# Pooled attention feeding a slot mixture of experts: idle products ahead of the scores dropped, second weights in 512 columns, half-width stores and loads joined

## The chip, the core and the metric

The kernel runs on one core of one Trainium2 chip. The metric is the device time of one execution in microseconds (us); before the change it is 179.56 us, the median of 3 runs (179.48 to 179.72). One further execution was recorded by the hardware profiler, and every duration below is from that record.

The names of the engines: PE is TensorE (PEld its weight loads), DVE is VectorE, ACT is ScalarE, POOL is GpSimd, SP is SyncE. POOL and SP here mostly issue DMAs: POOL the loads that cast f32 to bf16 on the way, SP the stores of the output.

## The reference

Two stages; only the second one's result is returned.

```python
def _attn_ref(q, k, v):                       # 8 batches, 8 heads, 576 rows, 64 columns, f32
    k_p = k.reshape(B, H, 72, 8, D).mean(axis=3)
    v_p = v.reshape(B, H, 72, 8, D).mean(axis=3)
    scores = scale * np.matmul(q, k_p.transpose(0, 1, 3, 2))
    attn = softmax over the 72 pooled keys
    return np.matmul(attn, v_p)

def _moe_ref(x, phi, w1, w2):                 # x 4608x512, 8 experts of 4 slots, w1 512x1024, w2 1024x512
    logits = x @ phi                          # 4608 x 32
    d = softmax of logits over the rows       # dispatch
    slot_input = d.T @ x                      # 32 x 512, four rows for each expert
    for e in range(E):
        slot_out[e] = np.maximum(slot_input[e] @ w1[e], 0.0) @ w2[e]
    c = softmax of logits over the slots      # combine
    return c @ slot_out                       # 4608 x 512
```

## The kernel before

**Batches go in four pairs.** For a pair, `load_pair` (L68 to L71) brings k, q and v into one tile each of 128 x 72 x 64 bf16. All twelve tiles share a pool of four buffers (tag `big`, L59), so the fifth load waits until the first tile has been read, and so on. The order of the loads is written out on POOL (`manual_schedule`, L66): k, q and v of pair 0, then of pairs 1 to 3 (L162 to L166), with w1 of expert 0 behind pair 2, then w1 of experts 1 to 7 (L167), then w2 of experts 0 to 3 into the same four `big` buffers (L169), w2 of experts 4 and 5 into the two buffers of the transposed q (L65 pool, issued at the end of pair 2), and last w2 of experts 6 and 7 into the two buffers of `xs` (`load_last_w2`, L85 to L96).

**PE's work on a pair.** `prepare_kq` pools k by products with `pmat` (L192), transposes q (L207) and folds the pooled k (L218). `prepare_v` pools v and carries it into the value tile (L256). `score_unit` makes the scores (L265) and ACT their exponentials (L266). `u_tile` multiplies by the values (L278), and DVE divides (L283, L284). `combine` makes the logits (L290), the slot inputs `G_ps` (L296) and the transposed combine weights `cT` (L311). The steps of the next pair's preparation are handed out one by one among the score units of the present pair. Until the last pair is done, the order on PE, ACT, DVE and SP is the tile framework's own; only POOL's is by hand.

**Idle products.** `warm(n, ps)` (L115) issues n products of 128x128 zeros with 128x512 zeros, whose result nobody reads. There are 18 of them at the top (L120), three times 4 among the steps of `prepare_kq(0)` (L341 to L344), seven in the last pair's logits, and 8 and 6 among the second weights (L508, L512).

**The last part** (from L388 on) has its order written out on PE, ACT, DVE and SP as well. The first weights give `hT`, a 128x32 weight block for each expert and each of eight row blocks, in which only the expert's own slots are not zero. `second(e, c)` (L470) then sums, for one expert and one half of 256 output columns, eight products, spread over four groups of 32 PSUM partitions; the two halves have a PSUM tile each (`so_ps`, L468). The second weights of experts 6 and 7 are loaded in column halves: five of eight row blocks of expert 6 in full width (L91), then for each half the other three row blocks of expert 6 (L94) and expert 7 in two DMAs of four row blocks each (L96).

**The output.** It is written by `output(g, cols)` (L479) in twelve groups: six of 256 rows (two per partition) and six of 512 rows (four per partition). The first five groups (`NHALF`) go in halves: as soon as column half 0 of the slot outputs is there (`slots_out(0)`, L477), its five groups are multiplied (L491), scaled by DVE for even and ACT for odd rows (L495, L493) and stored; then comes half 1. A store of a half row block (`w < DM`) is issued by SP for every row r by itself, 128 partitions of 1 KB (L498). The remaining seven groups are made in full width, one store each (L500): one of 512 KB and six of 1024 KB.

```python
        for r in range(n):
            f_ps = ...                                   # product, L491
            # scale into o_sb[:, r] on ACT (odd r) or DVE
            if w < DM:
                nc.sync.dma_start(out=dst[:, r], in_=o_sb[:, r])
        if w == DM:
            nc.sync.dma_start(out=dst, in_=o_sb)
```

Of the kernel before, what the change touches and what calls it, by code (L numbers as in the profile page):

```python
# [8 lines left out]
FP = mybir.dt.float32  # L9
BF = mybir.dt.bfloat16  # L10
AF = mybir.ActivationFunctionType
ALU = mybir.AluOpType
# [6 lines left out]
def kernel(  # L19
# [10 lines left out]
    nc = tc.nc  # L30
# [4 lines left out]
    DM = H * D  # L35
    E = moe_w1.shape[0]
    F = moe_w1.shape[2]
    NS = moe_phi.shape[1]
# [10 lines left out]
    FJ = F // 128  # L49
# [12 lines left out]
    ps_m = ctx.enter_context(tc.tile_pool(name="ps_m", bufs=2, space=PSUM))  # L62
# [15 lines left out]
    w2_sb = [None] * E  # L78
# [6 lines left out]
    def load_last_w2(pool, tag):  # L85

        j = FJ - 3
        src = [moe_w2[e].rearrange("(p j) d -> p j d", j=FJ) for e in range(E)]
        for e in (E - 2, E - 1):
            w2_sb[e] = pool.tile([128, FJ, DM], BF, name=f"w2_{tag}", tag=tag)  # L90
        nc.gpsimd.dma_start(out=w2_sb[E - 2][:, 0:j], in_=src[E - 2][:, 0:j])  # L91
        for c in range(2):
            cols = slice(c * DM // 2, (c + 1) * DM // 2)
            nc.gpsimd.dma_start(out=w2_sb[E - 2][:, j:FJ, cols], in_=src[E - 2][:, j:FJ, cols])  # L94
            for rows in (slice(0, FJ // 2), slice(FJ // 2, FJ)):
                nc.gpsimd.dma_start(out=w2_sb[E - 1][:, rows, cols], in_=src[E - 1][:, rows, cols])  # L96

    k_sb, q_sb, v_sb = [None] * NP, [None] * NP, [None] * NP

# [4 lines left out]
    hT = persist.tile([128, E, FJ, NS], BF)  # L104
# [10 lines left out]
    def warm(n, ps):  # L115
        for _ in range(n):
            nc.tensor.matmul(out=ps, lhsT=zeros[:, 0:128], rhs=zeros, start=True, stop=True)  # L117

    warm_ps = ps_m.tile([128, 512], FP, name="warm_ps", tag="m")
    warm(18, warm_ps)  # L120
    dummy = consts.tile([128, 1], BF)
    nc.scalar.activation(out=dummy, in_=zeros[:, 0:1], func=AF.Exp)

# [21 lines left out]
    for r in range(2):  # L145
        rows = slice(r * D, (r + 1) * D)
        nc.vector.tensor_copy(out=iphi[rows, :, 0:D],
                              in_=ident[rows, rows].rearrange("p d -> p () d").to_broadcast([D, H, D]))
# [8 lines left out]
    so = persist.tile([128, DM], BF)  # L157
    recC = persist.tile([128, 1], FP)
# [18 lines left out]
    ps_u = att.enter_context(tc.tile_pool(name="ps_u", bufs=2, space=PSUM))  # L177
# [5 lines left out]
    def pool_stage(src, dst):  # L183

        dst = dst.rearrange("p n (r i) -> p r n i", r=NR)
        for r0 in range(0, NR, 4):
            nr = min(4, NR - r0)
            ps = ps_m.tile([128, 4, BH, NI], FP, name="pool_ps", tag="m")
            for r in range(nr):
                for t in range(0, POOL, 2):  # L190
                    tt = (r0 + r) * POOL + t
                    nc.tensor.matmul(out=ps[:, r].rearrange("p n i -> p (n i)"),  # L192
                                     lhsT=src[:, tt:tt + 2, :].rearrange("p t d -> p (t d)"), rhs=pmat,
                                     start=(t == 0), stop=(t == POOL - 2))
            nc.scalar.copy(out=dst[:, r0:r0 + nr], in_=ps[:, 0:nr])  # L195
            yield

    def prepare_kq(pair):

        kpar = kvpool.tile([128, BH, SP], BF, name="kpar")  # L200
        yield from pool_stage(k_sb[pair], kpar)
        qT[pair] = qpool.tile([128, BH, NU, NI], BF, name="qT", tag="qT")
        for n, t0 in enumerate(range(0, NU, 6)):
            ps = ps_m.tile([128, 6, BH, NI], BF, name="q_ps", tag="m")
            for t in range(6):
                tt = 2 * (t0 + t)
                nc.tensor.transpose(out=ps[:, t].rearrange("p n i -> p (n i)"),  # L207
                                    in_=q_sb[pair][:, tt:tt + 2, :].rearrange("p t d -> p (t d)"), identity=ident)
            dst = qT[pair][:, :, t0:t0 + 6, :].rearrange("p n t i -> p t n i")
            if n % 3 == 1:  # L210
                nc.scalar.copy(out=dst, in_=ps)  # L211
            else:
                nc.vector.tensor_copy(out=dst, in_=ps)  # L213
            yield
        kp[pair] = kvpool.tile([128, BH, SP], BF, name="kp", bufs=2)
        for n in range(0, BH, HQ):
            ps = ps_m.tile([128, HQ, SP], FP, name="fold_ps", tag="m")
            nc.tensor.matmul(out=ps, lhsT=fold.rearrange("p r d -> p (r d)"), rhs=kpar[:, n:n + HQ],  # L218
                             start=True, stop=True)
            nc.vector.tensor_copy(out=kp[pair][:, n:n + HQ], in_=ps)  # L220
            if n % H:
                yield
# [115 lines left out]
        for g in gens:  # L338
            yield from g

    junk = ps_u.tile([128, 512], FP, name="junk", tag="u")  # L341
    for n, _ in enumerate(prepare_kq(0)):
        if n in (2, 5, 8):
            warm(4, junk)  # L344
    place_phi()

    comb = None
# [1 line left out]
    for pair in range(NP):  # L349
        for qd in range(2):  # L350
# [32 lines left out]
            if pair == NP - 1 and qd == 0:  # L383
                load_last_w2(xpool, "xs")
# [7 lines left out]
    junk = spare[:, 0]  # L392
# [26 lines left out]
    for n in range(E // NG):  # L419
        for half in range(F // 512):  # L420
            cols = slice(half * 512, (half + 1) * 512)
            h_ps = ps_m.tile([128, 512], FP, name="h_ps", tag="m")
            for j in range(DJ):
                for g in range(NG):
                    e = n * NG + g
                    nc.tensor.matmul(out=h_ps[g * NS:(g + 1) * NS],
                                     lhsT=siT[:, j, e * E:(e + 1) * E].rearrange("p e s -> p (e s)"),
                                     rhs=w1_sb[:, e, j, cols], start=(j == 0), stop=(j == DJ - 1),
# [17 lines left out]
    for n in [2] * NSMALL + [4] * ((NO - NSMALL) // 2):  # L446
        row0 = sum(128 * g[1] for g in groups)
        step_ = n // 2
        rows = lambda r, c0=row0 // 2, s=step_: cT[:, r % 2, c0 + r // 2:c0 + 128 * s:s]
# [14 lines left out]
    ps_o = ctx.enter_context(tc.tile_pool(name="ps_o", bufs=1, space=PSUM))  # L464
    ps_f = ctx.enter_context(tc.tile_pool(name="ps_f", bufs=4, space=PSUM))
    CW = DM // 2
    halves = [slice(c * CW, (c + 1) * CW) for c in range(2)]
    so_ps = [ps_o.tile([128, CW], FP, name=f"so_ps{c}") for c in range(2)]  # L468

    def second(e, c):  # L470
        for fj in range(FJ):
            g = fj % NG
            nc.tensor.matmul(out=so_ps[c][g * NS:(g + 1) * NS], lhsT=hT[:, e, fj], rhs=w2_sb[e][:, fj, halves[c]],  # L473
                             start=(e == 0 and fj < NG), stop=(e == E - 1 and fj >= NG), skip_group_check=True)

    def slots_out(c):
        nc.vector.tensor_scalar(out=so[:, halves[c]], in0=so_ps[c], scalar1=recC, scalar2=None, op0=ALU.mult)  # L477

    def output(g, cols):  # L479

        w = cols.stop - cols.start
        row0, n, rows = groups[g]
        dst = out[row0:row0 + 128 * n].rearrange("(p r) c -> p r c", r=n)[:, :, cols]
        if n == 4:

            o_sb = w1_sb[:, g - NSMALL].rearrange("p j f -> p (j f)").bitcast(FP).rearrange("p (r c) -> p r c", r=n)
        else:
            o_sb = opool.tile([128, n, w], FP, name=f"o_sb{w}", tag=f"o{w}", bufs=2 if w == DM else 2 * NHALF)
        for r in range(n):
            f_ps = ps_f.tile([128, w], FP, name="f_ps", tag="f")  # L490
            nc.tensor.matmul(out=f_ps, lhsT=rows(r), rhs=so[:, cols], start=True, stop=True)  # L491
            if r % 2:
                nc.scalar.activation(out=o_sb[:, r], in_=f_ps, func=AF.Copy, scale=recR[:, g, r:r + 1])  # L493
            else:
                nc.vector.tensor_scalar(out=o_sb[:, r], in0=f_ps, scalar1=recR[:, g, r:r + 1], scalar2=None,  # L495
                                        op0=ALU.mult)
            if w < DM:
                nc.sync.dma_start(out=dst[:, r], in_=o_sb[:, r])  # L498
        if w == DM:
            nc.sync.dma_start(out=dst, in_=o_sb)  # L500


    junk = ps_m.tile([128, 512], FP, name="junk", tag="m")
    for e in range(E - 2):
        for c in range(2):
            second(e, c)
        if e == E - 3:
            warm(8, junk)  # L508
    for c in range(2):
        second(E - 2, c)  # L510
        if c == 0:
            warm(6, junk)  # L512
        second(E - 1, c)
        slots_out(c)
        for g in range(NHALF):
            output(g, halves[c])
    for g in range(NHALF, len(groups)):
        output(g, slice(0, DM))
# [30 lines left out]
```

## Time and profile before

| what | value |
|---|---|
| median of 3 runs | 179.56 us (179.48 to 179.72) |
| the profiled execution | 179.56 us |
| its span, first to last instruction | 177.8 us, so 1.76 us lie around it |
| PE busy | 141.4 us (80%) |
| DVE, ACT, POOL busy | 91.1, 81.0, 19.7 us |
| loads through POOL's queue | 30.94 MB written as bf16, 6800 packets |
| stores and one small load through SP's queue | 9.50 MB, 4032 packets |
| HBM read, written | 61.93 MB, 9.44 MB |
| mean granted clock of TensorE | 0.835 |

How to read it: times on a line are microseconds from the start of the span. A line of the time-ordered view gives start, duration, engine, line of the kernel, operation, output and input tile and how many instructions are merged; in square brackets stands how long the engine was idle before and what ended that. In the table by stretches, the DMA share is the mean busy time of the core's 16 DMA engines (it can pass 1, as packets overlap), and GB/s counts bytes as they are written, so a load that casts f32 to bf16 counts half of what it reads.

### The profile page before, as it was taken

Reading aid. Unit: us, or ns where it says so; the run is one execution under the profiler, and the core shown is the slowest. Engines: PE = TensorE matmul, PEld = TensorE weight load, DVE = VectorE, ACT = ScalarE, POOL = GpSimd, SP = SyncE. Lnnn points to the kernel's source line nnn. Section 1 sums busy time; section 2 is a strip of 40 time slices with the busy share of each in tenths; the row PEclk is TensorE's granted clock in tenths of the full one; section 3 lists DMA queues with packets and bytes.
Section 4 is the critical chain, followed back from the end, with each engine's and each line's share of the span. In section 5 each row is a group of like instructions: output and inputs, shape, how many; then the busy total and the mean of one; then the engine's idle time right before and its main releaser. Section 6 shows DMA issues by size and latency. Waiting matters only on the chain.

```text
span 177.8 us, 3538 instructions
## 1 busy us (share of the span) xinstructions
PE 141.4 (80%) x1467; PEld 88.1 (50%) x1469; DVE 91.1 (51%) x252; ACT 81.0 (46%) x146; POOL 19.7 (11%) x39
## 2 busy tenths in 40 slices
PE   7983898799999999999999997798971486887000
PEld 2453576554986567865675444553660233322000
DVE  5401703446378787877868629843530006799000
ACT  3031389366595697856978813110200005599000
POOL 6010111002101160111111002103111000000000
PEclk9998799755699999999999567569998598589755
DMA  5999999999999999999999999999999999789994
GB/s 73 207 218 216 215 216 216 219 212 220 209 224 213 218 214 217 214 216 216 212 218 219 208 221 218 210 216 218 216 214 218 198 195 194 267 288 420 424 415 206
DMA packets 10846, 40.64 MB, mean 229 GB/s; under 512 B 976, under 2 KB 6480, under 8 KB 6736
## 3 DMA queue, kind: packets, MB, share of 16 engines
q0 software_dynamic: 6800, 30.94, 85.9%
q1 hardware_dynamic: 4032, 9.50, 13.8%
q8 instruction: 11, 0.18, 0.4%
q14 instruction: 3, 0.02, 0.0%
HBM read 61.93 MB, written 9.44 MB: 401 GB/s over the span
## 4 chain that ended last, share of the span: by engine, by line
PE 52%; DMA 24%; ACT 10%; DVE 4%; issue 2%; POOL 0%; ACTq 0%; DVEq 0%
DMA w_xs<-in_moe_w_dram 13%; DMA q_sb<-in_q_dram 11%; PE sc L265 8%; PE pool_ps L192 8%; PE u_ps L278 7%; PE G_ps L296 6%; PE q_ps L207 5%; PE f_ps L491 4%; PE warm_ps L117 4%; ACT w_sb L493 3%; DVE xs L284 2%; PE lg_ps L290 2%; PE fold_ps L218 2%; PE junk L117 1%; ACT ex_1632 L266 1%
## 5 line engine op out<-in xcount | busy, mean ns | idle before, releaser
L284 DVE TENSOR_TENSOR xs<-u_ps,rec 128x384 bf16<-128x384 f32 x72 | 39.4, 551 | 1.6
L265 PE MATMUL sc<-qT,kp 64*72 64x288 bf16 x128 | 24.5, 328 | 0.8 <-ACT ex_1633 L266 0.4
L283 DVE RECIPROCAL rec<-u_ps 128x4 f32<-128x4 f32 x72 | 12.4, 175 | 20.1 <-PE u_ps L278 19.8
L207 PE MATMUL q_ps<-ident,q_sb 128*128 128x128 bf16 x144 | 13.7, 249 | 5.3 <-DMA q_sb<-in_q_dram 5.0
L213 DVE COPY qT<-q_ps 128x768 bf16<-128x768 bf16 x16 | 8.8, 551 | 16.4 <-PE q_ps L207 16.3
L491 PE MATMUL f_ps<-so,cT 128*128 128x512 bf16 (+1 forms) x46 | 13.0, 385 | 2.8 <-DVE so L477 1.3
L207 PEld LDWEIGHTS <-q_sb 128*128 128x128 bf16 x144 | 10.4, 112 | 7.4 <-DMA q_sb<-in_q_dram 5.3
L265 PEld LDWEIGHTS <-kp 64*72 64x72 bf16 x128 | 8.9, 111 | 8.9 <-issue 3.5
L296 PE MATMUL G_ps<-xs,ee 128*128 128x512 bf16 x36 | 11.7, 468 | 0.4 <-ACT ee L291 0.4
L192 PE MATMUL pool_ps<-pmat,v_sb 128*128 128x128 bf16 x144 | 11.1, 239 | 0.0
L211 ACT COPY qT<-q_ps 128x768 bf16<-128x768 bf16 x8 | 6.4, 799 | 9.8 <-PE q_ps L207 9.7
L195 ACT CAST kpar<-pool_ps 128x512 bf16<-128x512 f32 (+1 forms) x12 | 5.5, 485 | 10.4 <-PE pool_ps L192 10.3
L491 PEld LDWEIGHTS <-cT 128*128 128x128 bf16 x46 | 4.8, 107 | 10.7 <-issue 7.9
L117 PEld LDWEIGHTS <-zeros 128*128 128x128 bf16 x51 | 5.6, 116 | 9.2 <-issue 5.0
L192 PEld LDWEIGHTS <-v_sb 128*128 128x128 bf16 x144 | 9.7, 109 | 0.8 <-issue 0.3
L493 ACT ACTIVATE o_sb_2313<-f_ps,recR 128x256 f32<-128x256 f32 x1 | 0.5, 474 | 20.5 <-PE f_ps L491 20.5
L192 PE MATMUL pool_ps<-pmat,k_sb 128*128 128x128 bf16 x144 | 9.7, 219 | 0.1
L192 PEld LDWEIGHTS <-k_sb 128*128 128x128 bf16 x144 | 8.4, 98 | 1.1 <-DMA k_sb<-in_k_dram 0.5
L495 DVE TENSOR_SCALAR w_sb<-f_ps,recR 128x512 f32<-128x512 f32 x12 | 8.3, 750 | 0.3 <-PE f_ps L491 0.2
L477 DVE TENSOR_SCALAR so<-so_ps_2183,recC 128x256 bf16<-128x256 f32 x1 | 0.5, 485 | 15.3 <-PE so_ps_2183 L473 15.3
L493 ACT ACTIVATE w_sb<-f_ps,recR 128x512 f32<-128x512 f32 x12 | 8.2, 687 | 0.2 <-PE f_ps L491 0.2
L195 ACT CAST vpar<-pool_ps 128x512 bf16<-128x512 f32 (+1 forms) x12 | 5.6, 480 | 5.7 <-PE pool_ps L192 5.6
(165 smaller groups left out, 238.8 us busy)
## 6 DMA issues: line engine op xcount, KB each, us to landing
w_sb<-in_moe_w_dram POOLq DMA_DIRECT2D x8, 1024.0 KB, 30.1
out_dram<-w_sb SPq DMA_DIRECT2D x6, 1024.0 KB, 8.9
k_sb<-in_k_dram POOLq DMA_DIRECT2D x4, 1152.0 KB, 17.8
q_sb<-in_q_dram POOLq DMA_DIRECT2D x4, 1152.0 KB, 17.9
v_sb<-in_v_dram POOLq DMA_DIRECT2D x4, 1152.0 KB, 16.3
w_big<-in_moe_w_dram POOLq DMA_DIRECT2D x4, 1024.0 KB, 38.4
w_qT<-in_moe_w_dram POOLq DMA_DIRECT2D x2, 1024.0 KB, 35.3
w_xs<-in_moe_w_dram POOLq DMA_DIRECT2D x4, 256.0 KB, 21.2
```

What stands on the lines that cost most here:

```text
L117: nc.tensor.matmul(out=ps, lhsT=zeros[:, 0:128], rhs=zeros, start=True, stop=True)
L192: nc.tensor.matmul(out=ps[:, r].rearrange("p n i -> p (n i)"), lhsT=src[:, tt:tt + 2, :].rearrange("p t d -> p (t d)"), rhs=pmat, start=(t ...
L195: nc.scalar.copy(out=dst[:, r0:r0 + nr], in_=ps[:, 0:nr])
L207: nc.tensor.transpose(out=ps[:, t].rearrange("p n i -> p (n i)"), in_=q_sb[pair][:, tt:tt + 2, :].rearrange("p t d -> p (t d)"), identity= ...
L213: nc.vector.tensor_copy(out=dst, in_=ps)
L265: nc.tensor.matmul(out=ps[:, r, 0:S // 2], lhsT=kp[pair][rows, n], rhs=qT[pair][rows, n], start=True, stop=True)
L278: nc.tensor.matmul(out=ps[rows, hh], lhsT=ex[b][:, hh].rearrange("p r t -> p (r t)")[:, c:c + rows.stop - rows.start], rhs=vp[(2 * pair + ...
L283: nc.vector.reciprocal(out=rec, in_=ps[:, :, XW])
L284: nc.vector.tensor_tensor(out=xs[pair][:, t, qd * HQ:(qd + 1) * HQ, :], in0=ps[:, :, 0:XW], in1=rec.rearrange("p h -> p h ()").to_broadcas ...
L296: nc.tensor.matmul(out=ps, lhsT=ee[:, t].rearrange("p g s -> p (g s)"), rhs=x[:, t, :, 0:D], start=(t == 0), stop=(t == 8))
L491: nc.tensor.matmul(out=f_ps, lhsT=rows(r), rhs=so[:, cols], start=True, stop=True)
L493: nc.scalar.activation(out=o_sb[:, r], in_=f_ps, func=AF.Copy, scale=recR[:, g, r:r + 1])
```

## The change

1. The 18 idle products at the top and the 12 among the steps of `prepare_kq(0)` are gone. The later ones stay.
2. `so_ps` becomes one tile of 128x512 f32. For experts 0 to 5 `second` multiplies all 512 columns with one product for each row block: 48 products in place of 96. Experts 6 and 7 go by halves, as before.
3. Expert 7's half columns come in one DMA of eight row blocks (512 KB) in place of two of four (256 KB each): two DMAs in place of four.
4. A half-width group of output rows is stored by one DMA with both rows (256 KB) once both are scaled, in place of one DMA for each row (128 KB): 10 stores in place of 20.

```diff
@@ load_last_w2
-            for rows in (slice(0, FJ // 2), slice(FJ // 2, FJ)):
-                nc.gpsimd.dma_start(out=w2_sb[E - 1][:, rows, cols], in_=src[E - 1][:, rows, cols])
+            nc.gpsimd.dma_start(out=w2_sb[E - 1][:, :, cols], in_=src[E - 1][:, :, cols])
@@
-    warm_ps = ps_m.tile([128, 512], FP, name="warm_ps", tag="m")
-    warm(18, warm_ps)
@@
-    junk = ps_u.tile([128, 512], FP, name="junk", tag="u")
-    for n, _ in enumerate(prepare_kq(0)):
-        if n in (2, 5, 8):
-            warm(4, junk)
+    for _ in prepare_kq(0):
+        pass
@@
-    so_ps = [ps_o.tile([128, CW], FP, name=f"so_ps{c}") for c in range(2)]
+    so_ps = ps_o.tile([128, DM], FP, name="so_ps")
-    def second(e, c):
+    def second(e, cols):
         for fj in range(FJ):
             g = fj % NG
-            nc.tensor.matmul(out=so_ps[c][g * NS:(g + 1) * NS], lhsT=hT[:, e, fj], rhs=w2_sb[e][:, fj, halves[c]],
+            nc.tensor.matmul(out=so_ps[g * NS:(g + 1) * NS, cols], lhsT=hT[:, e, fj], rhs=w2_sb[e][:, fj, cols],
@@ output
-            if w < DM:
-                nc.sync.dma_start(out=dst[:, r], in_=o_sb[:, r])
-        if w == DM:
-            nc.sync.dma_start(out=dst, in_=o_sb)
+        nc.sync.dma_start(out=out[row0:row0 + 128 * n].rearrange("(p r) c -> p r c", r=n)[:, :, cols], in_=o_sb)
@@
     for e in range(E - 2):
-        for c in range(2):
-            second(e, c)
-        if e == E - 3:
-            warm(8, junk)
+        second(e, slice(0, DM))
+    warm(8, junk)
     for c in range(2):
-        second(E - 2, c)
+        second(E - 2, halves[c])
         if c == 0:
             warm(6, junk)
-        second(E - 1, c)
-        slots_out(c)
+        second(E - 1, halves[c])
+        slots_out(halves[c])
```

More of the change, by code (lines that the diff above doesn't have):

```diff
@@ L467, with slots_out @@
     halves = [slice(c * CW, (c + 1) * CW) for c in range(2)]
-    so_ps = [ps_o.tile([128, CW], FP, name=f"so_ps{c}") for c in range(2)]
-    def second(e, c):
+    so_ps = ps_o.tile([128, DM], FP, name="so_ps")
+    def second(e, cols):
         for fj in range(FJ):
             g = fj % NG
-            nc.tensor.matmul(out=so_ps[c][g * NS:(g + 1) * NS], lhsT=hT[:, e, fj], rhs=w2_sb[e][:, fj, halves[c]],
+            nc.tensor.matmul(out=so_ps[g * NS:(g + 1) * NS, cols], lhsT=hT[:, e, fj], rhs=w2_sb[e][:, fj, cols],
                              start=(e == 0 and fj < NG), stop=(e == E - 1 and fj >= NG), skip_group_check=True)
-    def slots_out(c):
-        nc.vector.tensor_scalar(out=so[:, halves[c]], in0=so_ps[c], scalar1=recC, scalar2=None, op0=ALU.mult)
+    def slots_out(cols):
+        nc.vector.tensor_scalar(out=so[:, cols], in0=so_ps[:, cols], scalar1=recC, scalar2=None, op0=ALU.mult)
     def output(g, cols):
@@ L482, in output @@
         row0, n, rows = groups[g]
-        dst = out[row0:row0 + 128 * n].rearrange("(p r) c -> p r c", r=n)[:, :, cols]
         if n == 4:
```

## The prediction

> **What bounds the kernel now.** I read the page's 40 slices first. From the third microsecond to the end the DMA engines are busy, so the time is what they have to move, plus every stretch in which they move it slowly.
>
> ```profile
> PEclk9998799755699999999999567569998598589755
> DMA  5999999999999999999999999999999999789994
> GB/s 73 207 218 216 215 216 216 219 212 220 209 224 213 218 214 217 214 216 216 212 218 219 208 221 218 210 216 218 216 214 218 198 195 194 267 288 420 424 415 206
> ```
>
> A slice is 4.45 us. Up to slice 33 loads run at some 216 GB/s written. At the end stores run at 420. Between them two slices have only 267 and 288, and DMA falls from 9 to 7 and 8 tenths: a hole in the work of the bounding resource. The table by stretches gives its size (duration, busy time of PE, PEld, DVE, ACT, POOL, then granted clock, DMA share, GB/s):
>
> ```profile
> 149.00:158.30 9.30, 8.23 (x40) 3.21 (x40) 7.24 (x14) 6.47 (x13) 0.00 (x0) 0.63 0.80 259
> 159.00:165.00 6.00, 4.14 (x14) 1.25 (x13) 5.29 (x8) 5.42 (x8) 0.00 (x0) 1.00 1.01 410
> 165.00:175.50 10.50, 0.00 (x0) 0.00 (x0) 0.00 (x0) 0.00 (x0) 0.00 (x0) 0.58 1.01 421
> ```
>
> What holds it back is SP, in order of time:
>
> ```profile
> 148.56 0.82 SPq L498 DMA_DIRECT2D out_dram<-o_sb_2313  x2
> 149.42 0.94 SPq L498 DMA_DIRECT2D out_dram<-o_sb_2322  x2
> ...
> 156.38 0.89 SPq L498 DMA_DIRECT2D out_dram<-o_sb_2402  x2
> 157.36 0.90 SPq L498 DMA_DIRECT2D out_dram<-o_sb_2411  x2
> 158.36 0.39 SPq L500 DMA_DIRECT2D out_dram<-o_sb_2420  x1
> 158.91 6.29 SPq L500 DMA_DIRECT2D out_dram<-w_sb  x6
> ```
>
> Twenty half-width stores go out from 148.56 to 158.36, one every 0.49 us, without a pause. 131,072 bytes per 0.49 us are 267 GB/s: the rate of the hole. Two more rows say that SP is the limit, not the engines or the data: each store lands 1.9 to 2.2 us after its issue, the first as the last, so none queues; and the last half rows are scaled by 154.78, 3 us before SP sends them.
>
> **The loads have slack everywhere.** The list of POOL's waits shows loads held for PE, but a load waits behind others in the queue anyway:
>
> ```profile
> 39.90 0.53 POOL L70 DMA_DIRECT2D v_sb<-in_v_dram  x1 [9.07 <-PE q_ps L207]
> ...
> 61.58 0.53 POOL L70 DMA_DIRECT2D v_sb<-in_v_dram  x1 [7.46 <-PE sc L265]
> ...
> 121.97 1.55 POOL L96 DMA_DIRECT2D w_xs<-in_moe_w_dram  x2 [10.38 <-PE G_ps L296]
> ```
>
> The load ahead of the first (q of pair 2, issued 30.30, 18.4 to landing) lands at 48.7, that ahead of the second (q of pair 3, 53.59 + 17.4) at 71.0: PE could be 8.8 and 9.4 us later, less about 1 us until data flow, before the engines run dry. These are the smallest margins. Expert 7's loads, issued at 121.97, land 23.8 us later. So PE, at 80%, sets no end before 146.7, when the last piece of half 0 lands.
>
> **Idle products (part 1).** PE's own order in time:
>
> ```profile
> 1.19 6.57 PE L117 MATMUL warm_ps<-zeros 128*128 128x512 bf16 x18 [1.19 <-DVE ones L136]
> 7.60 2.75 PE L117 MATMUL junk<-zeros 128*128 128x512 bf16 x12
> 10.37 2.18 PE L192 MATMUL pool_ps<-pmat,k_sb 128*128 128x128 bf16 x36
> 15.84 0.84 PE L207 MATMUL q_ps<-ident,q_sb 128*128 128x128 bf16 x12 [3.28 <-DMA q_sb<-in_q_dram]
> ...
> 32.28 0.84 PE L207 MATMUL q_ps<-ident,q_sb 128*128 128x128 bf16 x12 [1.74 <-DMA q_sb<-in_q_dram]
> ```
>
> All 30 lie before 10.37, where k lands (issued 1.24, 9.1 to landing). Taking them away saves nothing; that wait is their cover. They do leave a fast PE: their weight loads start 0.43 us apart until 6.28 and 0.21 after. Without them the 36 pooling products run at the slow rate, as 32 of pair 1's v did at clock 0.50 (3.48 us, 0.109 each): 3.9 us in place of 2.2. The 1.7 us more go into the 3.28 us wait for q; the q load of pair 1, released by them, goes out at 14.6 in place of 12.85, where the load ahead lands at 26.7. Cost 0. If PE stays slow to 30.5, its some 9.4 us of busy time from 20 on double; less the 1.74 us wait at 32.28 it is 7.7 us late, still inside the margins.
>
> The Trainium skill, "TensorE: Matmul & The Clock Gate", Part 1, says that PE starts at half rate and is released after a busy window of about 3.4 us. Here it took 5.1 us of idle products. The rule speaks against the change; by it the slow time would be less than the row's, and both give 0 behind the wait.
>
> **Second weights (part 2).** Eight 256-column products take 0.22 us start to start at full clock (131.44 to 131.66), so sixteen take 0.44. Eight of 512 columns are in no row; bounds are 0.22 (a product costs its issue) and 0.44 (its columns); I take 0.44. Either way PE then waits 1.94 and 4.22 us for experts 4 and 5. One PSUM bank for both halves could make half 1's writes wait for DVE's reading of half 0; but ten output products stand between and need what DVE wrote, so no wait is added. Cost 0.
>
> **Expert 7 in one DMA per half (part 3).** POOL issues two fewer. The second piece today goes out 0.8 us after the first and lands 23.9 later, so the joined one lands with it, at 146.7. But four products that run before that (at 145.77) now come after: half of 0.22, so +0.11 us on half 0. On half 1 PE is busy with expert 6 until about 150.4, when the last piece lands (135.33 + 15.1): +0 to 0.2, inside the next sum's rounding.
>
> **Joined stores (part 4)** is what counts. SP's issue for two rows of 1 KB per partition is in no row: all stores here have one piece per partition, and cost 0.33 to 0.45 us whether 128 or 512 KB. Bounds: 0.49 pitch as now, or 0.98 if it goes by pieces. POOL's rows lean to the first: 128 pieces 0.54, 512 pieces (L96) 0.77. I take 0.55. For the rate of 1 KB pieces the ends are 268 / 0.80 = 335 GB/s (the hole, scaled to a full share) and 416 (the full-width stores); I take 335, the same piece.
>
> From issue to flow I take 0.85 us: the last half store is issued at 157.86, and the bytes after 159.0 add up to 6.87 MB, about the 6.82 MB of the full-width stores, so it had flowed by 159.1 with 0.3 to 0.4 for its own bytes.
> - Half 0: first pair scaled at 148.60 + 0.11, issued 148.8, flows from 149.65. Pairs follow every 0.45, so SP and data outrun the engines: 1.31 MB at 335 are 3.9 us, to 153.55.
> - Half 1: first pair scaled at 152.69 + 0.11, issued 152.85, flows from 153.7 to 157.6.
> - Group 5 (0.52 MB, scaled at 156.06): 157.6 + 1.26 = 158.9.
> - Six full stores: the first is scaled at about 157.6, so ready to flow at 158.55; 158.9 + 6.29 MB / 416 = 174.0.
>
> Now the flow ends at 175.5: **1.5 us less**. At 416 GB/s throughout, the scaling of the first full group is late next (158.55), and the end is 173.65: 1.85 less. The profiled execution took 179.56, the median itself, so 179.56 - 1.5 = 178.06; I say 178.0.
>
> The Trainium skill, "DMA: Bandwidth & Descriptors", section "Issuing engines are not separate DMA queues", calls the sequencer's time to start a DMA usually small beside the DMA. Here 0.49 us of SP stands against 0.39 us of engine time. By the rule joining would save nothing, 179.6.
>
> **Rivals.**
> - Less of it: PE's clock is lower at the end (half-width products were 0.52 apart at clock 0.5, 0.45 at 1.0), or fuller stores hold back the last load at 150.4. Each moves the first full group by up to 1 us: 178.6 to 179.2. Chance 0.11.
> - Joining saves no issue time: 0.98 per joined store. SP sends from 148.75, ten times 0.98, group 5 at 158.55 in place of 158.36: 179.7. For it: no row with two pieces. Against: POOL's rows. Chance 0.13.
> - Slower, by the clock: PE, never brought up, stays at half rate past 47. For: it was at 0.50 from 34 to 47 though busy throughout. It decides where v of pair 2 or 3 goes out over 8 us late. 7.7 late at 32, and each busy microsecond after 47 adds one; slow to 55 gives 7.7 + 8 - 8.4 = 7 us of empty engines, 178 + 7 = 185. Against: 5 us of dense products brought the clock up, and pair 1's v did so at 47. With smaller mishaps of this kind 0.11.
> - The forecast's own case, 177.0 to 178.6: 0.65.
>
> **How the numbers follow.** A measurement here tells about 0.2% from no change, so faster is under 179.2 and slower over 179.9. Faster 0.65 + 0.11 = 0.76, same 0.13, slower 0.11. The range goes from 177.0 (stores at 416 and half a microsecond earlier in flow) to 179.8, the no-gain case, and leaves out the slow clock.
>
> **What would show it.** Ten joined stores about 0.55 apart, landing later than 2 us (a queue); no 267 in the slices after the loads; the first full store issued near 157.7; the last load where it was, about 150.4; pooling of k at 0.109 each and q of pair 1 still landing by 32.3. Joined issues near 1 us, or a DMA share under 9 tenths between 10 and 140 us, would prove it wrong.

## The result, and the profile after

The changed kernel takes 179.0 us (median of 6 runs, 178.75 to 179.08) against 179.64 us of the kernel before (6 runs, 179.48 to 180.48): ratio 0.9949, 95% interval 0.9925 to 0.9974. So it is faster, by some 0.5%. Its profiled execution took 179.02 us, with a span of 177.2. The forecast was 178.0: the right side, the right mechanism for the stores, and a third to a half of the size; what took the rest was not in it.

The slices of the page after, to be read against those of before:

```profile
PEclk9999999655599999999999858558999569999655
DMA  4999999999999999999999999999999999999993
GB/s 73 210 221 210 223 208 224 208 224 208 223 207 215 219 218 214 219 215 209 218 220 211 211 226 215 209 215 224 213 209 223 197 196 152 343 348 416 424 422 137
```

The two slices of 267 and 288 GB/s have become 343 and 348, and DMA is at 9 tenths there. A new low, 152, stands just ahead of them. SP in order of time (start, duration):

```profile
148.76 0.61 SPq L491 DMA_DIRECT2D out_dram<-o_sb_2230  x1
149.46 0.56 SPq L491 DMA_DIRECT2D out_dram<-o_sb_2238  x1
...
154.27 0.61 SPq L491 DMA_DIRECT2D out_dram<-o_sb_2311  x1
154.98 0.98 SPq L491 DMA_DIRECT2D out_dram<-o_sb_2319  x1
...
156.06 1.37 SPq L491 DMA_DIRECT2D out_dram<-o_sb_2327  x1
157.61 6.26 SPq L491 DMA_DIRECT2D out_dram<-w_sb  x6
```

Ten stores where there were twenty, 0.67 us apart (0.58 of issue and 0.1 between). But the tenth and the one behind it hold SP for 0.98 and 1.37 us, and the first full store, whose last row had been scaled by 156.3, goes out at 157.61. The table by stretches (busy time of PE, PEld, DVE, ACT, POOL, then clock, DMA share, GB/s) shows two holes, at 149 and at 157:

```profile
149.00:150.00 1.00, 0.81 (x9) 0.33 (x11) 0.98 (x4) 0.97 (x3) 0.00 (x0) 1.00 0.22 30
...
155.00:157.00 2.00, 1.80 (x7) 0.63 (x7) 2.00 (x4) 1.80 (x4) 0.00 (x0) 1.00 1.03 343
157.00:158.00 1.00, 0.80 (x4) 0.28 (x4) 1.00 (x2) 1.00 (x2) 0.00 (x0) 1.00 0.74 263
158.00:165.00 7.00, 3.81 (x14) 1.08 (x12) 4.98 (x8) 4.72 (x8) 0.00 (x0) 1.00 1.03 421
```

In the kernel before the microsecond from 149 on moved 180 GB/s. So far that is the forecast's sum with some terms off. What it had no term for shows in the completions. Every store is spread over sixteen DMA engines, and the trace has sixteen completions for each, in order of time here:

```
completions of a store, us:      first    8th     15th    last engine
before, last full store          175.89  176.00  176.07  176.10
after, 6th joined store          154.90  154.98  155.05  155.08
after, 7th                       155.67  155.75  155.84  156.49
after, 8th                       156.40  156.49  156.60  158.38
after, 10th                      157.91  158.00  158.10  159.72
after, last full store           174.56  174.66  174.76  175.57
```

From the seventh joined store on, one completion of the sixteen, so one engine, is up to 1.8 us late, and at the end still 0.8. What was on it? The DMA view of 155.9 to 157.0 in the changed kernel (queue, packets, MB, share of 16 engines) has a packet that belongs to no tile:

```profile
q1 hardware_dynamic: 378, 0.36, 97.2%
q8 instruction: 1, 0.02, 5.5%
```

It begins at 155.93 and is 16 KB of instructions: 5.5% of sixteen engines over 1.1 us are 0.96 us of one engine. The kernel before has its last such packet at 143.66, among the loads:

```profile
q0 software_dynamic: 410, 0.20, 137.1%
q8 instruction: 1, 0.02, 5.5%
```

Both kernels have eleven of these packets while they run; the page of before has them as one line:

```profile
q8 instruction: 11, 0.18, 0.4%
```

Counted in TensorE's weight loads and products, they come 255 apart on average in the kernel before (215 begun at the first, 2768 at the last); no other engine has more than 252 instructions in all on that page. The experiments below that change nothing but TensorE's products move the last packet. The Trainium skill, "Runtime: NRT & Kernel Launch", section "Instruction fetch mechanics", says that an engine's instructions are refilled in blocks of 16 KiB, 256 instructions; the trace agrees. The changed kernel has 78 products fewer (30 idle ones and 48 of the second weights), 156 instructions of the 2936 on the page. So the last block falls due later in the work, at 155.93. The trace doesn't name the DMA engine that carries a packet: that the late engine is the one with the packet is inferred from the times, and from the runs below.

### The profile page after: what moved, and what is told of

Read it like the earlier page. It is cut to its first block, busy times and chain, and to the rows that moved or that the text cites. A ratio compares the mean times of both kernels' runs of the same rounds, so it can differ in the third digit from the quotient of the medians.

```text
span 177.2 us, 3367 instructions
## 1 busy us (share of the span) xinstructions
PE 134.0 (76%) x1389; PEld 85.8 (48%) x1391; DVE 91.0 (51%) x252; ACT 80.4 (45%) x146; POOL 18.5 (10%) x37
## 4 chain that ended last, share of the span: by engine, by line
PE 48%; DMA 28%; ACT 10%; DVE 4%; issue 2%; ACTq 0%; DVEq 0%; POOLq 0%
DMA w_xs<-in_moe_w_dram 13%; DMA q_sb<-in_q_dram 10%; PE pool_ps L189 10%; PE sc L262 8%; PE u_ps L275 8%; PE G_ps L293 6%; PE q_ps L204 5%; DMA k_sb<-in_k_dram 5%; PE f_ps L485 3%; ACT w_sb L487 2%; DVE xs L281 2%; PE fold_ps L215 2%; PE lg_ps L287 2%; ACT ex_1600 L263 1%; ACT ex_1601 L263 1%
## 5 line engine op out<-in xcount | busy, mean ns | idle before, releaser
L189 PE MATMUL pool_ps<-pmat,k_sb 128*128 128x128 bf16 x144 | 11.6, 242 | 10.1 <-DMA k_sb<-in_k_dram 10.0
L204 PE MATMUL q_ps<-ident,q_sb 128*128 128x128 bf16 x144 | 14.5, 258 | 3.9 <-DMA q_sb<-in_q_dram 3.5
L189 PEld LDWEIGHTS <-k_sb 128*128 128x128 bf16 x144 | 10.1, 110 | 10.6 <-DMA k_sb<-in_k_dram 10.0
L204 PEld LDWEIGHTS <-q_sb 128*128 128x128 bf16 x144 | 11.1, 117 | 6.2 <-DMA q_sb<-in_q_dram 3.9
L485 PE MATMUL f_ps<-so,cT 128*128 128x512 bf16 (+1 forms) x46 | 11.0, 331 | 3.5 <-DVE so L472 1.2
L485 PEld LDWEIGHTS <-cT 128*128 128x128 bf16 x46 | 4.3, 96 | 10.0 <-issue 7.6
L472 DVE TENSOR_SCALAR so<-so_ps,recC 128x256 bf16<-128x256 f32 x2 | 1.0, 482 | 14.1 <-PE so_ps L468 14.1
L217 DVE CAST kp<-fold_ps 128x288 bf16<-128x288 f32 x16 | 7.0, 441 | 1.6 <-PE fold_ps L215 1.5
```

## The experiments

**Theory A:** the joined stores bring some 1.6 us, and about 1 us of it is lost because the missing instructions move a fetch from the loads in among the stores, where each engine has its fixed share of the last bytes. **Rival B:** the joined stores bring what is measured, and the fetch costs nothing. **Rival C:** the gain is another part's.

**1. Joined stores alone** (part 4 on the kernel before):

```diff
-            if w < DM:
-                nc.sync.dma_start(out=dst[:, r], in_=o_sb[:, r])
-        if w == DM:
-            nc.sync.dma_start(out=dst, in_=o_sb)
+        nc.sync.dma_start(out=dst, in_=o_sb)
```

> The kernel before with part 4 alone: half-width rows joined into one store. Theory A (a 16 KB instruction fetch of PE, which moves with the number of PE instructions ahead of it, holds one DMA engine back among the last stores, and cost the changed kernel some 1 us): PE's list is untouched, so the last fetch stays at 143.7 us, ahead of the stores, and all sixteen engines finish the last store together. 177.8 to 178.3 us. Rival B (joined stores bring only what the changed kernel shows, and the fetch costs nothing): 179.0. Rival C (the gain came from the wide products or the joined loads): 179.6.

Measured 178.43 us (178.04 to 178.76), ratio 0.9917 (0.9895 to 0.9939). The last fetch is at 143.6, and the last store completes on its first and last engine at 174.28 and 174.50. One part of the change beats the whole by the medians, though the two intervals still overlap a little. It is 0.13 us above A's range, but all six runs lie below B and C.

**2. The 30 idle products put back** into the changed kernel (part 1 undone):

> The changed kernel with its 30 idle products put back (part 1 undone). 60 PE instructions more move the last fetch from 155.9 to some 149.9 us, where the engines stand nearly empty between the loads and the first joined store. A: 178.0 to 178.7. B, and whoever holds that idle products cost nothing in any way: 179.0.

Measured 179.02 us, with a wide range of 178.42 to 179.62 (10 runs), ratio 0.9948 (0.9928 to 0.9967). The fetch came at 150.72, not in the hole but on the first joined store, one of whose engines completes 1.7 us after the others, and the issue of the third store took 1.72 us. In the profiled execution, the slowest of the ten, the last load, too, landed late on one engine (150.97 in place of 150.3). The median is B's 179.0 and outside A's range: a miss for A, and with this spread no decision by itself.

**3. Instructions alone: 64 idle products of 32 columns** at the top of the changed kernel:

```diff
+    warm_ps = ps_m.tile([128, 512], FP, name="warm_ps", tag="m")
+    for _ in range(64):
+        nc.tensor.matmul(out=warm_ps[:, 0:32], lhsT=zeros[:, 0:128], rhs=zeros[:, 0:32], start=True, stop=True)
     dummy = consts.tile([128, 1], BF)
```

> The changed kernel with 64 idle products of 32 columns at the top, for their number of instructions alone: 128 more move the last fetch to some 145 us, among the last loads. A: 177.8 to 178.3, one engine no longer behind the others at the last store. B: 179.0.

Measured 178.03 us (177.85 to 178.36), ratio 0.9899 (0.9878 to 0.9919); run again as the base of the last three, 178.0 (0.992, 0.9901 to 0.9938). Work added on PE makes the kernel 1 us faster. The fetch is back among the loads (DMA view of 143.9 to 144.9):

```profile
q0 software_dynamic: 371, 0.19, 137.4%
q8 instruction: 1, 0.02, 5.8%
```

SP is no longer held, and the first full store goes out 0.9 us sooner than in the changed kernel:

```profile
148.89 7.65 SPq L494 DMA_DIRECT2D out_dram<-o_sb  x11
156.71 6.99 SPq L494 DMA_DIRECT2D out_dram<-w_sb  x6
```

All engines complete the last store between 174.39 and 174.61. The clock in the store stretch is 1.00 in both kernels up to 164.9, so a warmer PE is not the reason. Nor do the added products reach the stores by another way: the last load lands at 150.43 (150.31 in the changed kernel), and the first store goes out at 148.89 (148.76).

**4. Fewer instructions still**: the changed kernel without the seven idle products of the last pair's logits, and with expert 6's first five row blocks in 512 columns. The diff is abridged: `second` also gets the row blocks as a third argument.

```diff
-    warm(2, junk)      # twice, and warm(3, junk), among the last logits
+    second(E - 2, slice(0, DM), range(FJ - 3))
     for c in range(2):
-        second(E - 2, halves[c])
+        second(E - 2, halves[c], range(FJ - 3, FJ))
```

> The changed kernel with fewer PE instructions still: without the seven idle products of the last pair's logits, and the first five row blocks of expert 6 multiplied in 512 columns, 24 instructions less. A: the list ends before the last fetch falls due, or the fetch comes so late that it meets the last full-width stores; without it 177.8 to 178.3, with it 179.0 to 179.5. B: 179.0.

Measured 179.61 us (179.42 to 180.06), ratio 0.9993 (0.9979 to 1.0007): the whole gain is gone. The fetch fell at 162.2, among the full stores:

```profile
q1 hardware_dynamic: 52, 0.42, 102.6%
q8 instruction: 1, 0.02, 5.9%
```

Fifteen engines complete the last store by 174.53, as in experiment 3 (174.59), and the sixteenth at 176.18. The expected range, up to 179.5, is missed by 0.1 us. One more thing differs from experiment 3: PE's clock was 0.50 from 149.6 to 156.4 here and 1.00 there. But experiment 1 had the same low clock, from 149.8 to 156.7, and sent its stores at the same times. Stores and one stretch of experiment 1, then of experiment 4:

```profile
148.65 7.89 SPq L497 DMA_DIRECT2D out_dram<-o_sb  x11
157.67 7.17 SPq L497 DMA_DIRECT2D out_dram<-w_sb  x6
153.00:155.00 2.00, 1.92 (x7) 0.76 (x6) 1.47 (x4) 1.46 (x4) 0.00 (x0) 0.50 0.96 324
...
148.71 7.85 SPq L488 DMA_DIRECT2D out_dram<-o_sb  x11
157.58 7.94 SPq L488 DMA_DIRECT2D out_dram<-w_sb  x6
153.00:155.00 2.00, 1.92 (x7) 0.76 (x6) 1.47 (x4) 1.51 (x4) 0.00 (x0) 0.50 0.95 324
```

In experiment 1 the fifteenth engine completes the last store at 174.48 and the sixteenth at 174.50. So B falls here: with less work and the same stores, one engine alone is late, and the kernel is 1.2 us slower than experiment 1 and 1.6 us slower than experiment 3.

**5. Single rows again**, on experiment 3 (part 4 undone):

> The third experiment (64 short idle products, last fetch at 143.9 us) with the half-width rows stored one by one again (part 4 undone). If the joined stores are the whole gain: SP sends twenty stores 0.49 us apart again, the first full store goes out near 158.9, 179.4 to 179.8 us. If the wide products or the joined loads brought some of it: 178.5 to 179.2.

Measured 180.1 us (179.44 to 180.28), ratio 1.0012 (0.9999 to 1.0025). SP sends twenty stores 0.49 us apart and the first full one at 159.26. The time is 0.3 us above the range of the first case, and on its side: parts 1 to 3 without part 4 bring nothing, and C falls. The stretch reads as that of before:

```profile
153.00:155.00 2.00, 1.53 (x7) 0.58 (x6) 1.92 (x5) 1.79 (x5) 0.00 (x0) 1.00 0.80 268
155.00:157.00 2.00, 1.79 (x7) 0.63 (x7) 2.00 (x4) 1.80 (x3) 0.00 (x0) 1.00 0.80 268
```

**6. Parts 1 and 2 alone** on the kernel before:

> The kernel before with parts 1 and 2 alone (no idle products at the top, experts 0 to 5 in 512 columns). The last fetch moves to some 156 us, among single-row stores, which leave each DMA engine 20% idle. Theory A1 (a fetch costs only where its engine has no idle time left to catch up): 179.5 to 179.9. A2 (a fetch among the stores costs the same 1.1 us or more wherever it falls): 180.5 or more.

Measured 180.68 us (180.54 to 181.29), ratio 1.0054 (1.0036 to 1.0072). A1 was mine, and it fell; the time is in A2's range. The fetch came at 154.68, and the engines' spare fifth did not help, since SP, the bound there, was held itself: one store's issue took 1.51 us in place of 0.40. The late engine had caught up by the end (the last store completes between 177.04 and 177.25 on all), but every store behind went out later, the first full one at 160.08 in place of 158.91. The same stretch as above:

```profile
153.00:155.00 2.00, 1.58 (x7) 0.68 (x7) 1.92 (x4) 1.79 (x4) 0.00 (x0) 1.00 0.83 273
155.00:157.00 2.00, 1.80 (x7) 0.58 (x6) 2.00 (x4) 1.79 (x4) 0.00 (x0) 1.00 0.36 116
```

**7. 18 short idle products** in place of experiment 3's 64:

> The changed kernel with 18 short idle products at the top: 36 PE instructions more put the last fetch at some 152 us, amid the joined stores and earlier than the changed kernel's 155.9. Theory A: still in the stretch where all engines are full, so 178.9 to 179.7, one engine's landings behind the others. Rival B: 179.0 as the changed kernel, with no engine behind. If only fetches in the last 20 us count: 178.0.

Measured 178.55 us (178.34 to 179.04), ratio 0.9936 (0.9918 to 0.9953), below the range. The fetch came at 151.72; one engine was 1.9 us late and had made up all but 0.4 by the end. The other fifteen end at 174.85, 0.4 us later than in experiment 1, which had the same low clock in this stretch: from 153 to 155 the engines moved 260 GB/s here and 324 there. By the medians the fetch cost 0.5 us against experiment 3 and 0.1 against experiment 1, and the interval overlaps those of both. That an early fetch costs less is suggested by this, not shown.

**8. The first group row by row**, on experiment 3, to start the first flow sooner:

> The third experiment with the first group of half 0 alone stored row by row. The first joined store's bytes flowed 1.3 us after its issue, a single row's 0.85 us. If the slow start of joined stores costs what the engines' empty stretch from 149 to 150.2 suggests, 0.3 to 0.5 us: 177.5 to 177.8. If the time is made up later, or the first full store is what is late: 178.0.

Measured 178.27 us (177.82 to 178.69), ratio 0.9914 (0.9894 to 0.9935). Not faster than experiment 3. In the profiled execution the last load landed at 150.78 on one engine and the first store went out 0.3 us later, so what the slow start costs stays open.

**10. Expert 7's loads in two pieces per half**, on experiment 3 (part 3 undone), beside experiment 9, its repeat:

> The third experiment once more, as the base of the next three on the same chip: 178.0 us (177.8 to 178.4).

> The third experiment with expert 7's half columns loaded in two pieces each again (part 3 undone). By the working of part 3 the joined load costs 0.11 us on half 0, hidden or not: 177.9 to 178.1, no difference that can be told. If the joined load holds back the last landing: 177.6 or less. If joining helped: 178.3 or more.

Measured 178.38 us (178.04 to 178.66) against 178.0 (177.91 to 178.84); the intervals of the ratios, 0.9915 to 0.9944 and 0.9901 to 0.9938, overlap. The median is in the range named for a joined load that helps, but part 3 can't be told from nothing.

**11. No fetch at all:** experiment 4 with nine idle products less among the second weights.

```diff
-    warm(8, junk)
+    warm(2, junk)
-            warm(6, junk)
+            warm(3, junk)
```

> The fourth experiment with nine idle products less among the second weights (2 in place of 8, 3 in place of 6), 18 PE instructions fewer, so that the list ends before the fetch that fell at 162.2 us comes due. Theory A: no instruction packet after 134 us, all engines land the last store together, 177.9 to 178.5 in place of 179.6, though PE may be slower at the end. B, or if the missing instructions and not the fetch counted: 179.4 to 179.8.

Measured 178.93 us (178.23 to 179.6), ratio 0.9954 (0.9937 to 0.9971): 0.7 us less than experiment 4, not the 1.1 or more expected. The two intervals lie apart. The fetch is gone, and all engines complete the last store between 175.37 and 175.59. But PE had become slow: its clock was 0.50 from 141 to 158, half 0's first product started at 148.50 in place of 147.8, the first store went out at 149.68 (148.71 in experiment 4), and the engines stood empty longer. The other fifteen engines end 1.0 us later than in experiment 4 for it, and the sixteenth, no longer late, 0.6 us sooner. The empty stretch:

```profile
149.00:150.00 1.00, 0.99 (x5) 0.43 (x4) 0.93 (x3) 0.82 (x2) 0.00 (x0) 0.50 0.19 26
150.00:151.00 1.00, 0.99 (x5) 0.35 (x3) 0.90 (x2) 0.80 (x3) 0.00 (x0) 0.50 0.09 21
```

**12. Four groups in halves** in place of five, on experiment 3:

> The third experiment with four groups in halves in place of five. 1 KB pieces flow at 346 GB/s and full rows at 420, so two half stores fewer save 2 x 0.76 us and add 1.25 for a full store: 0.27 us less if the engines stay fed, 177.7 to 177.9. If half 0's four stores run out before half 1's first: 178.1 to 178.6.

Measured 178.7 us (178.15 to 179.15), ratio 0.9944 (0.9926 to 0.9961). The second case, 0.1 us above its range: from 153 to 155 the engines moved 203 GB/s, half 0's stores having run out. The clock was 0.50 there, which also made half 1 late; the two are not told apart.

The best version is experiment 3 at 178.0, 1 us below the changed kernel.

```
last fetch, us     joined stores   median us
143.6 to 143.9     exp. 1, 3, 9    178.43, 178.03, 178.0
150.7              exp. 2          179.02 (178.42 to 179.62)
151.7              exp. 7          178.55
155.9              changed kernel  179.0
162.2              exp. 4          179.61
```

## Why the prediction came out as it did

- **The bound and the rival "no issue time saved":** right. SP's twenty issues were the hole, and experiments 1 and 5 show that part 4 is all of the gain. A joined issue costs 0.67 us with its pause (taken: 0.55; ends 0.49 and 0.98).
- **Rate of 1 KB pieces:** 335 taken, 340 to 348 measured.
- **From issue to flow, 0.85 us:** failed in size. For a joined store it is 1.25 us (issue 148.76, flow from 150.01), hence the hole at 149.
- **Scaling of half 1 and group 5:** earlier than in the sum. The clock stayed at 1.00 until 165 where it had been 0.50 from 150 to 156, so half 1's first pair was scaled by 152.25 instead of 152.80 and the first full group by 156.3 instead of 157.7. The sum had no reason for this clock, and it is not what makes up for the hole: experiments 1 and 4 had the clock at 0.50 again, and their fifteen engines ended no later (174.48 and 174.53, here 174.76). The better rates do: 2.62 MB at 346 GB/s and 6.82 MB at 420 from 150.0 on end at 173.8 (an estimate from these figures), near the 174.0 of the sum; 174.76 less some 0.5 us from the end of flow to completion, as in the kernel before, is 174.3.
- **"Cost 0" of parts 1 and 2: this is the step that failed.** In PE's time they did cost nothing. Their cost was in what their instructions had held in place: without them the fetch landed among the stores and cost 179.0 - 178.03 = 1.0 us, the difference between 1.6 us of gain and 0.6 (against experiment 1, part 4 alone, it is 0.6 us). The forecast named a cover for PE's time and for SP's and POOL's queues, and none for the instruction queue, although its eleven packets stand on the page of before as a line of 0.4%.
- **The rivals' ranges:** 179.0 lies outside the forecast's own case (177.0 to 178.6) and inside that of the rival "less of it" (178.6 to 179.2), but for neither of its reasons: the clock at the end was higher, not lower, and the last load landed as before. That the first full store went out at 157.61, near the forecast's 157.7, is luck: its rows were ready at 156.3, and SP was held.
- **Slow start of PE:** as worked out. The pooling of k took 4.02 us from 10.02 on, the q load of pair 1 went out at 14.34 and landed at 32.3, the last slot inputs were 1.7 us later, and the loads ended as before. The rival "slower, by the clock" did not come about.
- **Part 3:** the joined piece put DVE's `so` 0.13 us later (147.26 for 147.13; taken 0.11), and the last load landed at 150.31 (150.38).

Left open: why a fetch of 0.95 to 1.45 us sets its engine back by 1.7 to 1.9 us, and what holds SP's issue when one engine is late. Nor do the runs settle why one engine's last load lands half a microsecond later in some executions; it may be part of the spread of the kernel before.

## What to carry to other kernels

When a change adds or removes instructions ahead of a stretch in which all DMA engines are full, look where the instruction packets fall in the new order: one block of 16 KB in such a stretch cost 1.0 us in the changed kernel and 1.6 us in experiment 4, against experiment 3, and some instructions more or fewer move it out. Compare the first and last engine's completion of the last store: a difference means that one engine had something else to do. And time a change's parts one by one, since here one part's gain paid for another part's side effect.

## What the runs showed of the hardware

- An instruction fetch is one packet of 16 KB, which took 0.89 to 0.98 us in the two kernels and 1.37 to 1.45 us among the stores of experiments 2, 6 and 7. One DMA engine is late behind it, and its share of the stores isn't taken over by the others: in experiment 4 they end at 174.53 and it at 176.18. The Trainium skill, "Runtime: NRT & Kernel Launch", section "Instruction fetch mechanics", says that the fetch is hidden behind the pace of issue. No run here tests whether PE waits for one; from the stores it is not hidden.
- SP's issue of a store with 256 pieces of 1 KB takes 0.53 to 0.67 us, with 128 pieces 0.34 to 0.47. Just behind a fetch single issues took 0.98 and 1.37 us (changed kernel), 1.72 (experiment 2) and 1.51 (experiment 6), but only 0.70 in experiment 7.
- Stores of 1 KB pieces reach some 345 GB/s, of 8 KB pieces 420.
